# Second expert layer: second products with the weights held still and all tokens of an expert moving

## The chip, the cores and the metric

The kernel runs on one core of a Trainium2 chip. TensorE (PE) multiplies: the fixed operand is loaded into the array first (its weight load, PEld), then the moving operand is streamed through it column by column, and the sums gather in one of eight banks. VectorE (DVE) and ScalarE (ACT) read those banks and write SBUF, GpSimd (POOL) issues the indirect transfers, and SyncE (SP) issues the loads of weights. Each engine works through its own instructions in the order in which they were issued and meets the others at semaphores. The metric is the device time of one execution in microseconds (us).

## The reference, cut to what matters

Attention over 4 x 12 heads gives 1792 tokens of 768 features, and a first expert layer transforms them. The second expert layer, which is what changes, gives every token to one of 8 experts, 224 tokens to each (`cap`), greedily by logit, and applies two products with a relu between them:

```python
    cap = N // E
    ...
    out = np.zeros((N, D), dtype=np.float32)
    for e in range(E):
        mask = assigned == e
        h = np.maximum(x[mask] @ w1[e], 0.0)
        out[mask] = h @ w2[e]
    return out.astype(np.float32)
```

Here N is 1792, D is 768 and the hidden width F is 1024.

## The kernel before

The second expert layer is the function `moe2`. It takes the experts one after the other. One expert has 32 steps (the loop over `t` at L2420): steps 0 to 15 are the first products, steps 16 to 31 the second ones.

**Tokens in.** The 224 tokens of an expert are gathered from `y` in two halves of 112 rows (`gather`, L2277, one indirect transfer each, on POOL) and turned by TensorE so that features lie on the partitions (`turn`, L2284 to L2300: 4 groups of 3 transposes, L2293, then copies on ACT, L2297, and DVE, L2300). The four groups are called g0 to g3 below; g0 and g1 are the first half of the tokens, g2 and g3 the second. The turned tokens are `xx`.

**First products.** A tile of w1 (128 x 128) is the fixed operand and all 224 tokens move. Experts 0 and 1 (`NAT` = 2) use plain 4-byte numbers, and TensorE makes two instructions of each such matmul (`acc`, L2308). Experts 2 to 7 use split numbers, a high and a low part of each operand: one matmul over 448 columns (tokens high and low, with the high weights, L2316) and one over 224 columns (tokens high, with the low weights, L2317), together `acc2`. The result goes through relu into `ht` (experts 0 and 1) or, by `relu2` (L2319 to L2329: ACT, DVE, ACT, DVE), into the high part `hh` and the low part `hl`.

**Second products.** `gemm2` (L2335) does it the other way round: the fixed operand is a piece of the hidden values (128 x 112 tokens), and 384 columns of w2 move. Per step it does two units; a unit is one plain matmul (L2345) or three split ones (L2348 to L2350). An expert has 32 units. The result has tokens on the partitions, so it is copied by ACT (L2355) and scattered to `out` by POOL (L2356) as it stands. The sums lie in three banks, `po3` = bank4, bank5 and bank6.

**Weights.** For experts 2 to 7 the weights come in 14 pieces each (6 of w1, 8 of w2) through a ring of 6 buffers (`qkv`). Each piece is split by `split` (L2266 to L2275): the high part by ACT (L2272, `w1h`, `w2h`), the low part by DVE (L2274, `w1l`, `w2l`). The splits of w1 for the next expert are done in the second phase of this one. Pieces 3 to 5 of an expert's w1 are held back (`LATE`, L2253 to L2257, a one-element MEMSET on POOL) until the gather of that expert's tokens has been issued.

**What sets the order.** The instruction order is written out by the program in advance: a planner (`Pace`, L1541) keeps an estimated clock for each engine, and the work that decides which tokens the next experts get (the assigner: many small instructions on PE, DVE and ACT, ending in `ids`, L2067) is put between the products where the planner's clocks have room. `ahead` (L2407) puts the gathers, turns and w1 splits of the next expert in where their planned inputs are there. The order is fixed when the program is built; an engine never takes a later instruction first.

Of the kernel before, what the change touches and what calls it, by code (L numbers as in the profile page):

```python
# [20 lines left out]
CP, NC = 112, 4  # L21
# [506 lines left out]
class Router:  # L528
# [15 lines left out]
    def init(self):  # L544
# [32 lines left out]
        self.i128 = pool.tile([CP, 1, 128], F32, name="i128")  # L577
# [141 lines left out]
    def first_slot(self, tb):  # L719

        nc, work = self.tc.nc, self.work
        na = (NB - 1) * NC
        shp = [CP, na, E]
        t = work.tile(shp, F32, name="fst")
        nc.vector.tensor_tensor(out=t, in0=self.oh[:, :na, :], in1=self.nst[:CP].to_broadcast(shp), op=OP.mult)
        p = work.tile([CP, na], F32, name="fsp")
        nc.vector.tensor_reduce(out=p, in_=t, axis=AX.X, op=OP.add)
        nc.vector.scalar_tensor_tensor(p, p, float(BIG), self.pl[:, :na], op0=OP.mult, op1=OP.add)
        os = []
        for n in range(NB + 1):  # L730
            yield
            if n < NB - 1:
                os.append([work.tile([CP, 128], F32R, name="fso", bufs=2 * NC) for _ in range(NC)])
                for j in range(NC):
                    nc.vector.tensor_scalar(os[n][j], self.i128[:, 0, :], p[:, n * NC + j : n * NC + j + 1], None, op0=OP.is_equal)
            m = n - 2
            for j in range(NC if m >= 0 else 0):
                nc.tensor.matmul(tb[:, 4 * m : 4 * m + 4], lhsT=os[m][j], rhs=self.tr[:, m * NC + j, :], start=j == 0, stop=j == NC - 1)
        yield
        t0 = work.tile([128, 1, 4], F32, name="t0")  # L740
        nc.vector.tensor_reduce(out=t0[:, 0, :], in_=tb.rearrange("p (n i) -> p i n", i=4), axis=AX.X, op=OP.add)
        self.slot0 = self.rows(1, t0[:, :, 0], (t0[:, :, 1], t0[:, :, 2]), "0")

    def slots(self, tb, room, ones):
# [76 lines left out]
        for j in range(na):  # L821
            o = ones[j][:CP] if j < len(ones) else work.tile([CP, 128], F32R, name="slo", bufs=3)
            if j in ON_ACT:

                sq = room[3][:CP, 128 * (j % 8) : 128 * (j % 8) + 128]
                nc.scalar.activation(sq, self.i128[:, 0, :], AF.Square, scale=-1.0, bias=lo[:, j : j + 1])
                nc.scalar.activation(o, sq, AF.Relu, scale=-1.0, bias=one)
            else:
                nc.vector.tensor_scalar(o, self.i128[:, 0, :], lo[:, j : j + 1], None, op0=OP.is_equal)
# [775 lines left out]
class Assigner:  # L1605
# [11 lines left out]
    def __init__(self, tc, consts, pool, bank, y, l2):  # L1617
# [27 lines left out]
        self.i128 = tile("i128a", [128, 128])  # L1645
        nc.gpsimd.iota(self.i128, pattern=[[1, 128]], base=0, channel_multiplier=0, allow_small_or_imprecise_dtypes=True)
# [517 lines left out]
def moe2(tc, consts, qkv, x0, asn, w1, w2, y, out):  # L2164
# [10 lines left out]
    with ExitStack() as ctx:  # L2175
# [11 lines left out]
        hl = p2.tile([128, KF, CAP], F32R, name="hl")  # L2187
        rows = {}
        zr = x0[0]
# [11 lines left out]

        def result(n, h, i):
            return po3[(4 * n + 2 * h + i) % 3][:CP, :384]
# [115 lines left out]
        def relu2(pg, f):  # L2319
            hr, hh = rows["hr"][f % NHR], rows["hh"]  # L2320
# [14 lines left out]
        def gemm2(n, h, t):  # L2335
            ts = slice(h * CP, (h + 1) * CP)

            todo = [(0, 0), (0, 1)] if t == 0 else [(1, 0), (1, 1)] if t == 1 else [(0, t), (1, t)]
            for i, k in todo:
                po = result(n, h, i)  # L2340
                work("p", 0.646 if n < NAT else 0.528, max(there[n, False, k], there["h", k]))
                cs = slice(384 * i, 384 * i + 384)
                ht, hh = rows["ht"], rows.get("hh")
                if n < NAT:
                    nc.tensor.matmul(po, lhsT=ht[:, k, ts], rhs=ws[n][1][:, k, cs], start=k == 0, stop=k == KF - 1)  # L2345
                else:
                    w2h, w2l = wh["2"]
                    nc.tensor.matmul(po, lhsT=hh[:, k, ts], rhs=w2h[:, k, cs], start=k == 0, stop=False)  # L2348
                    nc.tensor.matmul(po, lhsT=hh[:, k, ts], rhs=w2l[:, k, cs], start=False, stop=False)  # L2349
                    nc.tensor.matmul(po, lhsT=hl[:, k, ts], rhs=w2h[:, k, cs], start=False, stop=k == KF - 1)  # L2350

        def store(n, h):
            work("s", 0.98)
            for i in range(2):
                nc.scalar.activation(zr[:CP, 384 * i : 384 * i + 384], result(n, h, i), AF.Copy)  # L2355
            nc.gpsimd.indirect_dma_start(out=out, out_offset=IndirectOffsetOnAxis(ap=asn.ids[:, n, h : h + 1], axis=0), in_=zr[:CP], in_offset=None)  # L2356
# [10 lines left out]
        def experts(compact):  # L2367
# [28 lines left out]
            for n in range(E):  # L2396
                turns, gathered, turned = [], 0, 0

                def ahead(t):
# [7 lines left out]
                    elif t >= 17:  # L2407
# [9 lines left out]
                        if what[0] == n + 1 and (what[1] or n >= NAT and t > 25 and what[2] <= t - 25) and nload > nsplit + direct and arrival[what] <= clock["p"] + EARLY:  # L2417
                            split(*what)

                for t in range(32):  # L2420
# [10 lines left out]
                    if n and t == 3:  # L2431
                        store(n - 1, 1)
                    if t == 25:
                        store(n, 0)
# [19 lines left out]
                    else:  # L2454
                        gemm2(n, (t - 16) // 8, t % 8)
# [21 lines left out]
            store(E - 1, 1)  # L2477
# [15 lines left out]
NHR = 5  # L2493
# [5 lines left out]
NHR = 5  # L2499
# [7 lines left out]
ON_POOL = 4  # L2507
FEW = 7
# [3 lines left out]
def fused_kernel(tc, q, k, v, g_q, g_k, modality_id, w_gate, bias, w1, w2, w_gate2, w12, w22, out):  # L2512
    nc = tc.nc
    with ExitStack() as ctx:
# [13 lines left out]
        x0 = (xp.tile([128, DM], F32, name="x0"), xp.tile([128, KD, 128], F32R, name="xh"), xp.tile([128, KD, 128], F32R, name="xl"))  # L2528
# [40 lines left out]
```

## Time and profile before

| what | value |
|---|---|
| median of 3 runs (lowest, highest) | 993.45 us (989.86, 994.93) |
| the profiled execution | 989.51 us |
| its span, from the first to the last instruction | 987.6 us |
| mean granted TensorE clock, share of full speed | 0.994 |
| TensorE busy | 955.5 us, 97% of the span |
| VectorE busy | 655.4 us, 66% |
| ScalarE busy | 506.5 us, 51% |
| `moe2` | from about 665 us to the end |

The profile lists for each engine how long it was busy, what ended its idle time, and, in the trace, the start and length of every instruction. Matmuls overlap: the length of one is longer than the distance to the next, so costs on TensorE are read from the starts, not from the lengths. In the timelines P stands below for the start of an expert's first second product; the trace has P = 829.02 for expert 3, 862.58 for expert 4, 896.31 for expert 5 and 929.46 for expert 6.

### The profile page before, as it was taken

Reading aid. Unit: us, or ns where it says so; the run is one execution under the profiler, and the core shown is the slowest. Engines: PE = TensorE matmul, PEld = TensorE weight load, DVE = VectorE, ACT = ScalarE, POOL = GpSimd, SP = SyncE. Lnnn points to the kernel's source line nnn. Section 1 sums busy time; section 2 is a strip of 40 time slices with the busy share of each in tenths; the row PEclk is TensorE's granted clock in tenths of the full one; section 3 lists DMA queues with packets and bytes.
Section 4 is the critical chain, followed back from the end, with each engine's and each line's share of the span. In section 5 each row is a group of like instructions: output and inputs, shape, how many; then the busy total and the mean of one; then the engine's idle time right before and its main releaser. Section 6 shows DMA issues by size and latency. Waiting matters only on the chain. (4 is left out here: it accounts for less than half of the span.)

```text
span 987.6 us, 19357 instructions
## 1 busy us (share of the span) xinstructions
PE 955.5 (97%) x6241; PEld 774.6 (78%) x6241; DVE 655.4 (66%) x1693; ACT 506.5 (51%) x1158; POOL 306.8 (31%) x456
## 2 busy tenths in 40 slices
PE   7999999999999999999999999989999999999996
PEld 6666677677666688888888998747667799999996
DVE  6676877877965664444666554677778877687660
ACT  4787788788784422222441222741214466576651
POOL 4877776777632410100060111010110210220100
PEclk9999999999999999999999999999999999999999
DMA  7676577667465353728621111016932386767631
GB/s 164 144 159 165 145 167 175 152 161 173 97 194 183 113 210 113 252 88 303 231 84 34 34 65 38 18 47 248 343 126 80 117 274 217 251 209 243 217 114 31
DMA packets 81036, 152.55 MB, mean 154 GB/s; under 512 B 14270, under 2 KB 53438, under 8 KB 80768
## 3 DMA queue, kind: packets, MB, share of 16 engines
q1 hardware_dynamic: 73568, 127.57, 43.5%
q0 software_dynamic: 5200, 23.33, 7.4%
q8 instruction: 54, 0.88, 0.4%
q14 instruction: 86, 0.70, 0.2%
q10 hardware_dynamic: 2128, 0.07, 0.1%
HBM read 112.27 MB, written 17.44 MB: 131 GB/s over the span
## 5 line engine op out<-in xcount | busy, mean ns | idle before, releaser
L238 ACT ACTIVATE e<-sp,nm 112x448 f32<-112x448 f32 x192 | 123.6, 644 | 36.7 <-DVE nm L232 33.8
L232 DVE TENSOR_REDUCE nm<-sp 112x1 f32<-112x448 f32 x192 | 115.9, 616 | 27.5 <-PE sp L231 26.5
L1100 DVE CUSTOM_DVE_ANT_0 prod<-po,wgb,gt 128x384 bf16<-128x384 f32 x96 | 93.0, 969 | 37.8 <-ACT yr L1324 34.4
L246 PEld LDWEIGHTS tp<-ident,e 112*112 112x112 f32 x768 | 86.0, 134 | 38.8 <-DVE rs L277 6.3
L246 PE MATMUL tp<-ident,e 112*112 112x112 f32 x768 | 107.2, 262 | 3.6 <-ACT et L252 3.5
L2316 PE MATMUL bank<-xx,w1h 128*128 128x448 f32 x288 | 92.6, 378 | 0.0
L252 ACT ACTIVATE et<-tp 112x448 f32<-112x448 f32 x142 | 78.2, 551 | 16.6 <-PE tp L246 16.6
L230 PE MATMUL sp<-bt,at 128*112 128x448 f32 x188 | 82.9, 441 | 0.8 <-DMA bt<-cut 0.8
L1036 PE MATMUL po<-w2h,hh 128*128 128x384 f32 x224 | 78.9, 352 | 0.1
L2356 POOL DMA_INDIRECT out_dram<-x,ids x16 | 16.4, 1024 | 200.4 <-ACT x L2355 166.5
L1013 PE MATMUL pg<-w1h,xh 128*128 128x512 f32 x180 | 75.0, 417 | 3.0 <-ACTq L970 2.1
L259 PE MATMUL op<-et,qkv 112*64 112x448 f32 x384 | 77.5, 545 | 0.0
L2317 PE MATMUL bank<-xx,w1l 128*128 128x224 f32 x288 | 76.5, 265 | 0.0
L1037 PE MATMUL po<-w2l,hh 128*128 128x384 f32 x224 | 75.2, 336 | 0.1
L1038 PE MATMUL po<-w2h,hl 128*128 128x384 f32 x224 | 75.2, 336 | 0.0
L1014 PE MATMUL pg<-w1l,xh 128*128 128x512 f32 x180 | 71.2, 396 | 0.0
L1015 PE MATMUL pg<-w1h,xl 128*128 128x512 f32 x180 | 71.2, 395 | 0.0
L231 PE MATMUL sp<-bt,qz 128*112 128x448 f32 x188 | 69.2, 368 | 0.0
L2348 PE MATMUL bank<-w2h,hh 128*112 128x384 f32 x192 | 66.3, 345 | 0.0
L2350 PE MATMUL bank<-w2h,hl 128*112 128x384 f32 x192 | 64.7, 337 | 0.0
L2349 PE MATMUL bank<-w2l,hh 128*112 128x384 f32 x192 | 64.6, 337 | 0.0
L1136 POOL DMA_INDIRECT y<-yr,ti x11 | 11.4, 1039 | 161.3 <-POOLq L970 113.4
(485 smaller groups left out, 2277.0 us busy)
## 6 DMA issues: line engine op xcount, KB each, us to landing
qkv<-in_moe_w_dram SPq DMA_DIRECT2D x88, 384.0 KB
qkv<-in_moe_w_dram SPq DMA_DIRECT2D x36, 512.0 KB
raw<-in_moe_w_dram SPq DMA_DIRECT2D x24, 512.0 KB
bt<-cut SPq DMA_DIRECT2D x96, 112.0 KB
at<-cut SPq DMA_DIRECT2D x96, 112.0 KB
w1s<-in_moe_w_dram SPq DMA_DIRECT2D x12, 512.0 KB
w2s<-in_moe_w_dram SPq DMA_DIRECT2D x16, 384.0 KB
qkv<-in_v_dram SPq DMA_DIRECT2D x12, 448.0 KB
```

Source lines behind the costliest of these rows:

```text
L230: nc.tensor.matmul(sp, lhsT=at[:, h, cs], rhs=bt[:, h, :], start=True, stop=False)
L232: nc.vector.tensor_reduce(out=st["nm"][:, n : n + 1], in_=sp, axis=AX.X, op=OP.max, negate=True)
L238: nc.scalar.activation(e, st.pop(("s", n)), AF.Exp, bias=st["nm"][:, n : n + 1], accum_out=st["sm"][:, n : n + 1])
L246: nc.tensor.transpose(tp[:, kc, :], e[:, kc * CP : (kc + 1) * CP], ident[:CP, :CP])
L252: nc.scalar.activation(dst, tp, AF.Copy)
L259: nc.tensor.matmul(st["op"][h * D : (h + 1) * D, :], lhsT=raws[i // 2][:, 2, 2 * (i % 2) + h, kc * D : (kc + 1) * D], rhs=st["et"][:, h, k ...
L1036: nc.tensor.matmul(po[n], lhsT=hh[:, k, :], rhs=w2h[:, kk, cs], start=kk == 0, stop=False)
L1037: nc.tensor.matmul(po[n], lhsT=hh[:, k, :], rhs=w2l[:, kk, cs], start=False, stop=False)
L1038: nc.tensor.matmul(po[n], lhsT=hl[:, k, :], rhs=w2h[:, kk, cs], start=False, stop=kk == KF - 1)
L1100: nc.vector.tensor_tensor_reduce(out=prod, in0=y, in1=wgb[:, cs, e], scale=gt, scalar=init[:, e : e + 1] if init is not None else 0.0, op0 ...
L2316: nc.tensor.matmul(pg, lhsT=h[:, k, fs], rhs=xx[:, k].rearrange("p a c -> p (a c)"), start=k == 0, stop=False)
L2317: nc.tensor.matmul(pg[:, :CAP], lhsT=l[:, k, fs], rhs=xh[:, k, :], start=False, stop=k == KD - 1)
```

## The change

For experts 0 to 6 the second product is turned round: a 128 x 128 tile of w2 is the fixed operand, and all 224 tokens move (`second`), in 48 units per expert (6 blocks of 128 output features, d, by 8 pieces of the hidden width, k), three units per step, in the order `UNITS`. A unit is one plain matmul over 224 columns, or for split experts one over 448 columns (`hh` and `hl` now lie side by side in one tile, `hx`) and one over 224. Each block d fills one bank of `po3`, `po3[d % 3]`, for its 8 units.

The result then has features on the partitions. `leave` copies it to `yt`: ACT alone for experts 0 and 1; for split experts ACT copies one half of the sum to a small buffer `hr` and DVE adds the other half from the bank. The bank is free for block d + 3 only after that. `back` turns `yt` on TensorE into rows of tokens (4 groups of 3 transposes per expert: two in steps 28 and 30, two in steps 4 and 6 of the next expert), and `keep` copies them by ACT and scatters them. Blocks 4 and 5 leave in the next expert's step 0. The last expert keeps `gemm2`. Splits of w2 for the next expert are let in by `FREE2` in place of a fixed step, the ring of `hr` has 3 buffers in place of 5, there are two `zr` for the rows on their way out, and one constant (`i128`) is shared.

```diff
-        def gemm2(n, h, t):
+        def gemm2(h, t):
...
+        def second(n, d, k):
+            ds = slice(128 * d, 128 * d + 128)
+            po = po3[d % 3]
+            flags = dict(start=k == 0, stop=k == KF - 1)
+            done["y", d] = work("p", 0.388 if n < NAT else 0.318, max(there[n, False, k], there["h", k]))
+            if n < NAT:
+                nc.tensor.matmul(po[:, :CAP], lhsT=ws[n][1][:, k, ds], rhs=rows["ht"][:, k, :], **flags)
+            else:
+                w2h, w2l = wh["2"]
+                hx = rows["hx"][:, k]
+                nc.tensor.matmul(po[:, : 2 * CAP], lhsT=w2h[:, k, ds], rhs=hx.rearrange("p a c -> p (a c)"), start=k == 0, stop=False)
+                nc.tensor.matmul(po[:, :CAP], lhsT=w2l[:, k, ds], rhs=hx[:, 0], start=False, stop=k == KF - 1)
+
+        def leave(n, d):
+            po, to = po3[d % 3], yt[:, d]
+            if n < NAT:
+                work("s", 0.36, done["y", d])
+                nc.scalar.activation(to, po[:, :CAP], AF.Copy)
+                return
+            hr = rows["hr"][d % NHR]
+            t = work("s", 0.36, done["y", d])
+            nc.scalar.activation(hr, po[:, CAP : 2 * CAP], AF.Copy)
+            work("v", 0.39, t)
+            nc.vector.tensor_tensor(out=to, in0=po[:, :CAP], in1=hr, op=OP.add)
+
+        def back(h, i, px):
+            work("p", 0.33)
+            for k in range(3):
+                nc.tensor.transpose(px[:CP, 128 * k : 128 * k + 128], yt[:, 3 * i + k, h * CP : (h + 1) * CP], ident)
+
+        def keep(n, h, i, px):
+            work("s", 0.49)
+            nc.scalar.activation(zr[h][:CP, 384 * i : 384 * i + 384], px[:CP, :384], AF.Copy)
+            if i:
+                nc.gpsimd.indirect_dma_start(out=out, out_offset=IndirectOffsetOnAxis(ap=asn.ids[:, n, h : h + 1], axis=0), in_=zr[h][:CP], in_offset=None)
...
-                        if what[0] == n + 1 and (what[1] or n >= NAT and t > 25 and what[2] <= t - 25) and nload > nsplit + direct and arrival[what] <= clock["p"] + EARLY:
+                        if what[0] == n + 1 and (what[1] or n >= NAT and t > FREE2[what[2]]) and nload > nsplit + direct and arrival[what] <= clock["p"] + EARLY:
...
-                        gemm2(n, (t - 16) // 8, t % 8)
+                        if n + 1 == E:
+                            gemm2((t - 16) // 8, t % 8)
+                        else:
+                            for u in range(3 * t - 48, 3 * t - 45):
+                                second(n, *UNITS[u])
...
-NHR = 5
+NHR = 3
...
+UNITS = [(2 * j + d, k) for j in range(3) for d, k in [(0, 0), (0, 1), (1, 0), (1, 1)] + [(d, k) for k in range(2, 6) for d in range(2)] + [(0, 6), (0, 7), (1, 6), (1, 7)]]
+LEAVES = [u // 3 + 1 for d in range(6) for u in (UNITS.index((d, 7)),)]
+FREE2 = [16 + max(UNITS.index((d, k)) for d in range(4, 6)) // 3 for k in range(8)]
+TURNED, TURNED2 = (28, 30), (4, 6)
```

The rows below are instructions as they stand on one engine, in order; `waits` names the engines whose semaphores an instruction waits for.

TensorE, expert 3, second phase, before: two units around the turn group g2 (xg1).

```order
L2348 MATMUL bank5_11540<-w2h_12740,hh_12745 112x384
L2349 MATMUL bank5_11540<-w2l_12741,hh_12745 112x384
L2350 MATMUL bank5_11540<-w2h_12740,hl_11544 112x384
L2293 MATMUL bank7_11542<-ident_71,xg1_11546 128x112 [waits DMASW3_49,DVE_49]
L2293 MATMUL bank7_11542<-ident_71,xg1_11546 128x112 x2
L2348 MATMUL bank4_11539<-w2h_12740,hh_12745 112x384
```

The same place after: units 15 to 19; bank6 is block d = 2, and the second bank4 is block d = 3.

```order
L2289 MATMUL bank7_11540<-ident_71,xg1_11545 128x112 [waits DMASW2_49,DVE_49]
L2289 MATMUL bank7_11540<-ident_71,xg1_11545 128x112 x2
L2355 MATMUL bank5_11538<-hx_12803,w2h_12798 128x448
L2356 MATMUL bank5_11538<-hx_12803,w2l_12799 128x224
L2355 MATMUL bank6_11539<-hx_12803,w2h_12798 128x448
L2356 MATMUL bank6_11539<-hx_12803,w2l_12799 128x224
L2355 MATMUL bank6_11539<-hx_12803,w2h_12798 128x448
L2356 MATMUL bank6_11539<-hx_12803,w2l_12799 128x224
L2355 MATMUL bank4_11537<-hx_12803,w2h_12798 128x448 [waits DVE_49]
L2356 MATMUL bank4_11537<-hx_12803,w2l_12799 128x224
```

Unit 18, the first of block 3, now waits for a DVE instruction, the one that empties bank4 of block 0.

VectorE, expert 3, second phase, before: the splits of the next expert's w1 (w1l) and its turned tokens (xx).

```order
L2274 TENSOR_TENSOR w1l_12328<-qkv1_87,w1h_12327 128x1024
L2300 TENSOR_TENSOR xx_11543<-bank7_11542,xx_11543 128x3x112
L2274 TENSOR_TENSOR w1l_12328<-qkv1_87,w1h_12327 128x1024
L2274 TENSOR_TENSOR w1l_12328<-qkv0_86,w1h_12327 128x1024
L2300 TENSOR_TENSOR xx_11543<-bank2_11537,xx_11543 128x3x112
L2274 TENSOR_TENSOR w1l_12328<-qkv0_86,w1h_12327 128x1024 x2
```

The same place after.

```order
L2270 TENSOR_TENSOR w1l_12348<-qkv1_87,w1h_12347 128x1024
L2296 TENSOR_TENSOR xx_11541<-bank7_11540,xx_11541 128x3x112
L2270 TENSOR_TENSOR w1l_12348<-qkv1_87,w1h_12347 128x1024
L2270 TENSOR_TENSOR w1l_12348<-qkv0_86,w1h_12347 128x1024
L2296 TENSOR_TENSOR xx_11541<-bank2_11535,xx_11541 128x3x112
L2270 TENSOR_TENSOR w1l_12348<-qkv0_86,w1h_12347 128x1024
L2368 TENSOR_TENSOR yt_11543<-bank4_11537,hr0_12804 128x224
L2270 TENSOR_TENSOR w1l_12348<-qkv0_86,w1h_12347 128x1024
L2368 TENSOR_TENSOR yt_11543<-bank5_11538,hr1_12805 128x224
```

The add that empties bank4 (the first yt, L2368) stands behind four w1l and two xx.

VectorE, the numbers of expert 7's tokens (ids), before: amid expert 5's first products, between the hr and hl of its relu.

```order
L2324 TENSOR_TENSOR hr0_12746<-bank7_11542,hr0_12746 128x224
L2329 SCALAR_TENSOR_TENSOR hl_11544<-hr0_12746,hh_12745 128x224
L2063 TENSOR_TENSOR table_11116<-table_11116,bank1_11536 112x32
L2064 TENSOR_TENSOR sel_11155<-table_11116,full_11105 112x32
L2065 TENSOR_REDUCE sum4_11156<-sel_11155 112x4
L2067 TENSOR_TENSOR ids_11118<-sum4_11156 112x2
L2324 TENSOR_TENSOR hr1_12747<-bank2_11537,hr1_12747 128x224
```

After: in expert 6's second phase, the whole stretch from the first three w1l on.

```order
L2270 TENSOR_TENSOR w1l_12348<-qkv1_87,w1h_12347 128x1024 x2
L2270 TENSOR_TENSOR w1l_12348<-qkv0_86,w1h_12347 128x1024
L2368 TENSOR_TENSOR yt_11543<-bank4_11537,hr0_12804 128x224
L2368 TENSOR_TENSOR yt_11543<-bank5_11538,hr1_12805 128x224
L2062 TENSOR_TENSOR table_11116<-table_11116,bank1_11534 112x32
L2063 TENSOR_TENSOR sel_11153<-table_11116,full_11105 112x32
L2064 TENSOR_REDUCE sum4_11154<-sel_11153 112x4
L2066 TENSOR_TENSOR ids_11118<-sum4_11154 112x2
L2368 TENSOR_TENSOR yt_11543<-bank6_11539,hr2_12806 128x224
L2368 TENSOR_TENSOR yt_11543<-bank4_11537,hr0_12804 128x224
L2296 TENSOR_TENSOR xx_11541<-bank7_11540,xx_11541 128x3x112
L2270 TENSOR_TENSOR w1l_12348<-qkv0_86,w1h_12347 128x1024
```

The ids moved from the first phase of one expert to the second phase of the next, behind three w1l; likewise the ids of expert 6 moved from expert 4's first phase to expert 5's second one. The gathers, the turns and pieces 3 to 5 of w1 follow them.

TensorE at the end of expert 6's second phase, before: the last unit and expert 7's first products.

```order
L2348 MATMUL bank4_11539<-w2h_12740,hh_12745 112x384
L2349 MATMUL bank4_11539<-w2l_12741,hh_12745 112x384
L2350 MATMUL bank4_11539<-w2h_12740,hl_11544 112x384
L2316 MATMUL bank2_11537<-xx_11543,w1h_12327 128x448 [waits DVE_49]
L2317 MATMUL bank2_11537<-xx_11543,w1l_12328 128x224
```

After: the last units, g2 and g3, and expert 7's first products.

```order
L2355 MATMUL bank6_11539<-hx_12803,w2h_12798 128x448
L2356 MATMUL bank6_11539<-hx_12803,w2l_12799 128x224
L2289 MATMUL bank7_11540<-ident_71,xg1_11545 128x112 [waits DMASW0_49,DVE_49]
L2289 MATMUL bank7_11540<-ident_71,xg1_11545 128x112 x2
L2289 MATMUL bank2_11535<-ident_71,xg1_11545 128x112 [waits DVE_49]
L2289 MATMUL bank2_11535<-ident_71,xg1_11545 128x112 x2
L2312 MATMUL bank2_11535<-xx_11541,w1h_12347 128x448 [waits DVE_49]
L2313 MATMUL bank2_11535<-xx_11541,w1l_12348 128x224
```

Here g2 and g3 stand behind all second products, directly ahead of the first product that reads them; before, all four groups stood between units in the first half of the phase.

## Rows read from the trace of the kernel before

**Rows 1.** Page of the profile, part 1: busy time, share of the span, instructions.

```profile
PE 955.5 (97%) x6241; PEld 774.6 (78%) x6241; DVE 655.4 (66%) x1693; ACT 506.5 (51%) x1158; POOL 306.8 (31%) x456
```

**Rows 2.** Waits of TensorE, 665 to 990 us: in total, times, longest us.

```profile
PE bank L2293 <- DMA xg<-y,ids: 2.0, 2, 1.1
PE bank L2293 <- DVE hl L2329: 0.8, 1, 0.8
```

**Rows 3.** Timeline of TensorE, expert 6, where its phases start: start us, us, line.

```profile
929.46 0.34 PE L2348 MATMUL bank<-w2h,hh 128*112 128x384 f32 x1
...
947.43 0.36 PE L2316 MATMUL bank<-xx,w1h 128*128 128x448 f32 x1
...
962.61 0.34 PE L2348 MATMUL bank<-w2h,hh 128*112 128x384 f32 x1
```

**Rows 4.** Timeline of TensorE, transposes between second products of experts 2 and 1.

```profile
773.57 0.81 PE L2345 MATMUL bank<-w2s,ht 128*112 128x384 f32 x2
774.22 0.49 PE L1824 MATMUL bank<-ident,bid 128*128 128x128 f32 x3
774.54 0.81 PE L2345 MATMUL bank<-w2s,ht 128*112 128x384 f32 x2
...
797.08 0.34 PE L2350 MATMUL bank<-w2h,hl 128*112 128x384 f32 x1
797.26 0.45 PE L2293 MATMUL bank<-ident,xg 112*128 112x112 f32 x3
...
797.72 0.34 PE L2349 MATMUL bank<-w2l,hh 128*112 128x384 f32 x1
```

**Rows 5.** Timeline of TensorE, plain products of experts 0 and 1.

```profile
689.01 3.65 PE L2308 MATMUL bank<-xtt,w1s 128*128 128x224 f32 x18
692.49 0.49 PE L2060 MATMUL bank<-place,g 128*112 128x32 bf16 x7
...
758.50 2.75 PE L2345 MATMUL bank<-w2s,ht 128*112 128x384 f32 x8
761.08 0.45 PE L2293 MATMUL bank<-ident,xg 112*128 112x112 f32 x3
```

**Rows 6.** Timeline of VectorE, second phase of expert 6.

```profile
931.90 1.23 DVE L2274 TENSOR_TENSOR w1l<-qkv,w1h 128x1024 fp32r<-128x1024 f32 x1 [0.56 <-ACT w1h L2272]
...
933.46 2.35 DVE L2274 TENSOR_TENSOR w1l<-qkv,w1h 128x1024 fp32r<-128x1024 f32 x2
...
936.15 2.35 DVE L2274 TENSOR_TENSOR w1l<-qkv,w1h 128x1024 fp32r<-128x1024 f32 x2
938.41 0.50 DVE L2300 TENSOR_TENSOR xx<-bank,xx 128x336 fp32r<-128x336 f32 x1
```

**Rows 7.** Groups of instructions, 672 to 988 us: busy us, mean ns, idle before.

```profile
L2272 ACT ACTIVATE w1h<-qkv 128x1024 fp32r<-128x1024 f32 x36 | 36.6, 1051 | 0.0
...
L2324 DVE TENSOR_TENSOR hr<-bank,hr 128x224 f32<-128x224 f32 x48 | 18.7, 390 | 17.1 <-ACT hr L2322 17.0
L2322 ACT ACTIVATE hr<-bank 128x224 f32<-128x224 f32 x48 | 17.2, 359 | 32.7 <-PE bank L2317 32.6
```

**Rows 8.** Timeline of VectorE, expert 7's numbers in expert 5's first phase.

```profile
893.91 0.18 DVE L2063 TENSOR_TENSOR table<-table,bank 112x32 f32<-112x32 f32 x1
...
894.59 0.16 DVE L2067 TENSOR_TENSOR ids<-sum 112x2 int32<-112x2 f32 x1
```

**Rows 9.** Landing of two gathers (663.4, 916.2 us), and POOL's timeline around the second.

```profile
DMA to landing us min/median/max: 3.7/3.7/3.7
...
DMA to landing us min/median/max: 7.0/7.0/7.0
...
916.16 0.97 POOL L2282 DMA_INDIRECT xg<-y,ids  x1 [0.16 <-issue]
...
918.39 0.09 POOL L2257 MEMSET qkv<- 1x1 f32 x1
```

**Rows 10.** Stretch by stretch: PE, PEld, DVE, ACT, POOL busy, clock, DMA share, GB/s.

```profile
922.00:926.00 4.00, 4.00 (x28) 3.77 (x27) 1.57 (x4) 1.58 (x5) 0.00 (x0) 1.00 1.00 332
```

More of the change, by code (lines that the diff above doesn't have):

```diff
@@ L2342, in gemm2 @@
                 cs = slice(384 * i, 384 * i + 384)
[L2343 to L2356, printed above, removed]
+                hh, hl = rows["hx"][:, k, 0, ts], rows["hx"][:, k, 1, ts]
+                nc.tensor.matmul(po, lhsT=hh, rhs=w2h[:, k, cs], start=k == 0, stop=False)
@@ new lines, in gemm2 @@
+                nc.tensor.matmul(po, lhsT=hh, rhs=w2l[:, k, cs], start=False, stop=False)
+                nc.tensor.matmul(po, lhsT=hl, rhs=w2h[:, k, cs], start=False, stop=k == KF - 1)
+        def second(n, d, k):
[6 more added lines that the diff above has]
+            else:
+                w2h, w2l = wh["2"]
+                hx = rows["hx"][:, k]
+                nc.tensor.matmul(po[:, : 2 * CAP], lhsT=w2h[:, k, ds], rhs=hx.rearrange("p a c -> p (a c)"), start=k == 0, stop=False)
+                nc.tensor.matmul(po[:, :CAP], lhsT=w2l[:, k, ds], rhs=hx[:, 0], start=False, stop=k == KF - 1)
@@ new lines, in keep, with results @@
+        def keep(n, h, i, px):
[3 more added lines that the diff above has]
+                nc.gpsimd.indirect_dma_start(out=out, out_offset=IndirectOffsetOnAxis(ap=asn.ids[:, n, h : h + 1], axis=0), in_=zr[h][:CP], in_offset=None)
+        def results(n, t):
+            if n + 1 < E and t in TURNED:
+                back(TURNED.index(t), 0, pg2[1])
+            if n + 1 < E and t - 1 in TURNED:
+                keep(n, TURNED.index(t - 1), 0, pg2[1])
+            if n + 1 < E and t - 16 in LEAVES:
+                leave(n, LEAVES.index(t - 16))
+            if n and t + 16 in LEAVES[4:]:
+                for d in range(4, 6):
+                    if LEAVES[d] == t + 16:
+                        leave(n - 1, d)
+            if n and t in TURNED2:
+                back(TURNED2.index(t), 1, po3[TURNED2.index(t)])
+            if n and t - 1 in TURNED2:
+                keep(n - 1, TURNED2.index(t - 1), 1, po3[TURNED2.index(t - 1)])
@@ L2430, in experts @@
                         next(sums, None)
[L2431 to L2434, printed above, removed]
+                    results(n, t)
+                    if n + 1 == E and t == 25:
+                        for i in range(2):
+                            keep(n, 0, i, po3[i])
                     ahead(t)
@@ L2464, in experts @@
                     wh["2"] = tiles(1, "right", *((i, (KF, DM), F32R) for i in ("w2h", "w2l")))
-                    rows["hh"], *rows["hr"] = tiles(1, "right", ("hh", (KF, CAP), F32R), *((f"hr{i}", (CAP,), F32) for i in range(NHR)))
+                    rows["hx"], *rows["hr"] = tiles(1, "right", ("hx", (KF, 2, CAP), F32R), *((f"hr{i}", (CAP,), F32) for i in range(NHR)))
                 while known <= n + 1:
@@ L2476, in experts @@
                     split(*piece(nsplit + direct))
-            store(E - 1, 1)
+            for i in range(2):
+                keep(E - 1, 1, i, po3[(2 + i) % 3])
             for r in room:
@@ L2498 @@
 FIRST = 1
-NHR = 5
+NHR = 3
 LATE = 3
```

25 lines of the change are left out of this document (11 added, 14 removed).

## Prediction

> **What bounds the kernel now.** I read the busy times first: TensorE is busy for 97% of the span, VectorE for 66%, ScalarE for 51% [rows 1]. Then the waits of TensorE in the expert layer that changes: 2.8 us in all between 665 and 990 us, in three pieces [rows 2]. So here TensorE's own instructions set the time, and every microsecond taken from them counts, as long as nothing makes TensorE wait; every new wait counts in full too. The third view is the timeline of one split expert: its second phase runs from 929.46 to 947.43 us, its neighbour's first products from there to 962.61 [rows 3]. Those two stretches give the prices of the old and of the new form, since the new second products have the shapes of the first ones (a 128 x 128 tile held, 448 and 224 columns moving).
>
> **What is removed and added on TensorE.** The 48 first pairs take 962.61 - 947.43 = 15.18 us, 0.316 each [rows 3]. The second phase takes 17.97 us; it holds 4 turn groups of three transposes. One such group stands between the starts 797.08 and 797.72 together with two matmuls; at the ordinary distance of 0.175 (525 ns per unit of three) that leaves 0.64 - 0.35 = 0.29 for the group [rows 4]. Without them 17.97 - 4 x 0.29 = 16.8 us remain, 32 units of 0.525. So a split expert's second products go from 16.8 to 15.2 us, a gain of 1.6; for experts 2 to 6 that is 8.1.
>
> For the plain experts, where a matmul is two instructions, 8 instructions of the old form take 761.08 - 758.50 = 2.58 us, 0.3225 per instruction and 0.645 per unit; 18 instructions of the first products take 3.48 us, 0.193 each and 0.387 per matmul [rows 5]. 32 x 0.645 = 20.6 becomes 48 x 0.387 = 18.6: a gain of 2.1 each, 4.2 for experts 0 and 1. The whole gain is 12.3 us.
>
> The turning back adds 7 x 4 = 28 groups of three transposes against the 4-byte identity. The nearest row is a group of three of the same kind and width (128 moving columns) between plain products: from 773.57 to 774.54 with two products of 0.3225 in it, so 0.97 - 0.645 = 0.32 [rows 4]; the narrower groups (112 columns) gave 0.29. I take 0.32: 28 x 0.32 = 9.0 us (8.1 to 9.2). TensorE's own work thus falls by 12.3 - 9.0 = 3.3 us.
>
> The Trainium skill, "TensorE: Matmul & The Clock Gate", section "Back-to-back issue gap", gives a distance of N/2.4 + 2.5 ns for an isolated matmul of N columns at the full clock; it also says that in a stream the weight loads count. By that formula an old split unit would take 0.488 and a new pair 0.285 us, where the rows show 0.525 and 0.316. The gain per split expert would be 1.9 in place of 1.6, the sum 1.6 us lower; I go by the rows.
>
> **What is moved to other engines.** ACT gets, per split expert, 6 copies out of the banks of 0.36 [rows 7] and keeps its 4 row copies; DVE gets 6 adds of 0.39 [rows 7]. Neither engine is full over a whole expert, so as busy time I cost them at nothing. What counts is their place in the queue, as the block that fills a bank for the second time waits for the add that emptied it.
>
> **The first new wait: bank4, unit 18.** Unit 18 opens block 3 in the bank of block 0 and waits for DVE. On DVE the add of block 0 stands behind the fourth split of the next expert's w1 in experts 2, 3 and 4. In the trace of expert 6, which has the same string of splits and turned tokens before the change as those, the first split starts 2.44 us after P (929.46), the fourth at 936.15, and two take 2.26, so the fourth ends at P + 7.82 [rows 3, 6]. The add ends at P + 8.2, and TensorE goes on at P + 8.3. It arrives earlier: 18 units of 0.316 and three turn groups of 0.29 are 6.56. So it waits for 1.75 us in experts 3 and 4. In expert 2 the wait for `hl` of 0.8 [rows 2] makes it arrive later, so 0.95. In experts 5 and 6 only three splits stand ahead: the add is done by P + 6.2, TensorE is there at 5.7 to 6.0 with a few small products of the assigner between, and waits for about 0.3. Together 0.95 + 3.5 + 0.6 = 5.05. The bounds: no wait, if the splits ran some 1.8 us earlier than now (they start when ACT's `w1h` is done [rows 6], and nothing in the change moves that), and 6.5 if experts 2, 5 and 6 paid more. The later banks have room: bank6 for block 5 is the tightest, some 0.1 us.
>
> **The second new wait: the next expert's tokens, experts 5 and 6.** The planner counts the new adds on DVE and so puts the assigner's last steps later. The `ids` of expert 7, now amid expert 5's first products at 894.59 [rows 8], come in expert 6's second phase behind three splits and two adds: P + 2.44 + 3 x 1.13 + 2 x 0.39 + the 0.84 from `table` to the end of `ids` [rows 6 to 8] = P + 7.5. The two gathers follow; 2.2 us after the first the gate for pieces 3 to 5 of w1 opens [rows 9], at P + 9.9. What a transfer then needs is not shown for this place. In a quiet queue a gather landed after 3.7 us, in one shared with weight loads after 7.0 [rows 9]. At P + 7.5 the queue of weights is held at the gate, so I take 3.7 for the first gather: it lands at P + 11.4, and TensorE wants it at about P + 12.0. With 3.7 for the first of the three held pieces too, and 0.52 MB at 332 GB/s [rows 10] = 1.55 for each more, the last lands at P + 16.7; then ACT splits it for 1.05 [rows 7] and DVE for 1.22 [rows 6], to P + 19.0. Behind that, by the order, comes the DVE step for g2 (0.5), without which expert 7's first product can't start: P + 19.6. TensorE is done with the second products and all its transposes at 15.2 + 1.9 (6 groups: two back, four in) + 0.3 = P + 17.4. The wait is 2.2, and by the same steps 2.0 for expert 5 (`ids` earlier by one add, one w2 split more ahead of g2). I take 2.1 each, 4.2 together. Its bounds are 1.2 each, if the pieces land as they are wanted and only DVE's order counts, and about 4 each with the landing of 7.0, where TensorE already stops at g0 (P + 7.2 + 7.0 = 14.2 against 10.8 in expert 5).
>
> Other moves at nothing: the stores are issued by POOL behind gathers that have no hurry, and `out` is stored later by some steps, but expert 7 keeps the old end. Three `hr` buffers serve a chain of 0.85 us per block. The back transposes in the next expert's steps 4 and 6 come more than 1 us after block 5's add.
>
> **The sum.** -12.3 + 9.0 + 5.05 + 4.2 = +5.95 us. On the profiled execution (989.51, span 987.6) that is 995.5. The median of the runs shown is 993.45, 3.9 above the profiled one; the forecast is made for the median: 999.4.
>
> **The rivals.**
> *No new wait.* If DVE reaches the add before TensorE reaches unit 18 (P + 6.56; it needs to be 1.75 us ahead of the trace) and the next tokens come in time, only TensorE's own work counts: -3.3, 990.1 us. This is the one that ends on the other side, though within 0.5%. For it: with the same splits on DVE TensorE waits for only 2.8 us now. Against: the splits' times are measured, and the order puts the add behind them.
> *Only the bank waits.* If the held pieces and the gathers land early, or DVE's order has more slack at the expert's end than I see: -3.3 + 5.05 = +1.75, 995.2.
> *A late gather.* At the landing of 7.0 both experts 5 and 6 pay about 4 in place of 2.1: +9.8, 1003.2. For it: the row at 916.16 stands ahead of the same gate. Against: there the loads of w1 ran beside it, which now come later.
> *Dear transposes.* The same page of the Trainium skill, section "Part 4: PE-mode transpose", gives about 275 ns for a transpose in a kernel's context and says that such work doesn't count toward the clock. At 0.275 each in place, 84 transposes cost 23.1 in place of 9.0: +20, 1013.5. The rows speak against it: three between products took 0.29 to 0.32 in all [rows 4].
>
> **How the numbers follow.** The forecast with both waits, 997 to 1002, has 0.48; only the bank waits 0.20; no new wait 0.10; a late gather 0.15; dear transposes 0.02; something below all of them 0.05. A measurement of this kernel tells about 0.5% (5 us) from no change. Faster by more than that, below 988.5, is 0.06. Within it lie the two cheap cases and the lower edge of the forecast (up to 998.4): 0.38. Slower has 0.56. The range from 991.0 to 1004.5 leaves out the no-wait case and the dearest ones, about 2 in 10.
>
> **What would show it.** Right: pairs of second products 0.316 apart; turn-back groups costing 0.32; unit 18 of experts 3 and 4 waiting about 1.75 us for the first `yt` add behind the fourth w1l; the first product of experts 6 and 7 waiting about 2 us for `xx`. Wrong: TensorE's waits in the layer staying near 2.8 us, w1l starting earlier than P + 2.4, or g0 of experts 6 and 7 waiting for its gather.

## The result, and the profile after

The changed kernel takes 1003.88 us (median of 6 runs, 1002.17 to 1006.51) against 993.26 us (median of 6) before on the same chip. These medians lie 10.6 us apart; the ratio given with the result is 1.0134, with an interval of 1.0113 to 1.0154, which is 13 us. It is slower, as forecast, but by 11 to 13 us, not by 6. The profiled execution took 1002.17 us with a span of 1000.3.

The page of the kernel after, part 1, and TensorE's waits from 660 to 1000 us (in total, times, longest us), which answer to [rows 1, 2]. Waits and phases, here and below, are read from one trace of each kernel:

```profile
PE 957.7 (96%) x6389; PEld 790.7 (79%) x6389; DVE 663.1 (66%) x1723; ACT 514.3 (51%) x1200; POOL 304.6 (30%) x455
```

```profile
PE bank L2312 <- DVE xx L2296: 5.0, 2, 2.7
PE bank L2355 <- DVE yt L2368: 4.1, 3, 1.5
PE bank L2373 <- ACT x L2377: 1.5, 1, 1.5
PE bank L2289 <- DVE xx L2296: 1.4, 1, 1.4
PE bank L2289 <- DMA xg<-y,ids: 1.3, 2, 1.1
```

TensorE is busy for hardly longer, but waits for 13.3 us where it waited for 2.8. Four kinds of wait are new: the first product of experts 6 and 7 for `xx`, unit 18 for the `yt` add, a turn-back group (L2373) for ACT's copy of the one ahead, and a turn group (L2289) for `xx`.

Where the time went is read best from the starts of the phases. The table gives the length of each phase in us, from its first product to the first product of the next; F are first and S second products, e1 and e2 two of the experiments below.

| phase | before | after | e1_early_ids | e2_spread |
|---|---|---|---|---|
| experts 0 and 1, S | 29.39, 25.09 | 26.64, 23.33 | 26.64, 23.33 | 26.64, 23.32 |
| expert 2, F and S | 15.30, 19.35 | 16.26, 18.66 | 16.26, 20.79 | 16.24, 19.29 |
| expert 3, F and S | 16.83, 17.97 | 17.71, 18.67 | 15.95, 18.89 | 15.83, 17.77 |
| expert 4, F and S | 15.59, 18.13 | 15.95, 18.80 | 16.25, 19.02 | 15.83, 17.43 |
| expert 5, F and S | 15.60, 17.96 | 15.84, 22.62 | 16.25, 18.79 | 15.84, 17.04 |
| expert 6, F and S | 15.19, 17.97 | 17.38, 22.21 | 15.84, 18.79 | 15.83, 17.03 |
| expert 7, F and S | 15.19, 25.02 | 18.01, 24.91 | 15.84, 24.90 | 15.83, 25.08 |
| from expert 0's first product to the end | 315.1 | 328.2 | 318.8 | 310.2 |

Up to the end of expert 4 the changed kernel is a little ahead: expert 5 starts at 879.35 in place of 880.71 us. From expert 5's second phase on it loses 14 us, in four phases.

The timeline of TensorE after (start us, us, engine, line, operation, and in brackets the idle time before it with what ended it), around the end of expert 5:

```profile
907.48 0.38 PE L2355 MATMUL bank<-hx,w2h 128*128 128x448 f32 x1
907.69 0.27 PE L2356 MATMUL bank<-hx,w2l 128*128 128x224 f32 x1
907.80 0.38 PE L2355 MATMUL bank<-hx,w2h 128*128 128x448 f32 x1
...
912.28 0.54 PE L2373 MATMUL bank<-ident,yt 128*112 128x128 f32 x3 [1.49 <-ACT x L2377]
...
917.81 0.74 PE L2312 MATMUL bank<-xx,w1h 128*128 128x448 f32 x1 [2.33 <-DVE xx L2296]
...
918.53 0.60 PE L2312 MATMUL bank<-xx,w1h 128*128 128x448 f32 x1
918.93 0.39 PE L2313 MATMUL bank<-xx,w1l 128*128 128x224 f32 x1
919.12 0.60 PE L2312 MATMUL bank<-xx,w1h 128*128 128x448 f32 x1
...
921.56 0.38 PE L2312 MATMUL bank<-xx,w1h 128*128 128x448 f32 x1
```

A pair of second products takes 0.32 us, as foreseen. Then come a wait of 1.49 and, at the start of expert 6's first products, one of 2.33; and behind it the pairs stand 0.59 apart (918.53 to 919.12) until about 921. That is not a wait. The stretches say what it is (busy time of each engine, granted clock, DMA share, GB/s):

```profile
894.00:917.60 23.60, 19.79 (x132) 17.59 (x131) 16.29 (x46) 12.69 (x22) 1.99 (x3) 1.00 0.53 181
917.80:921.00 3.20, 3.19 (x11) 2.98 (x12) 2.29 (x4) 0.48 (x2) 0.00 (x0) 0.50 0.97 331
921.20:934.60 13.40, 13.40 (x89) 12.72 (x88) 9.60 (x20) 8.97 (x21) 2.89 (x3) 1.00 0.48 157
...
957.40:961.80 4.40, 4.40 (x15) 4.10 (x16) 3.26 (x6) 1.54 (x5) 0.00 (x0) 0.50 0.90 308
```

The granted clock is 0.50, the lower of its two levels (1.2 in place of 2.4 GHz), from 917.6 to 921.0 and again from 955.1 to 961.9: the first time as the wait of 2.33 ends, the second from within the wait of 2.71 at the next expert's end, 0.9 us behind one of 1.40. In the kernel before it is 1.00 all through these phases.

What held expert 6's tokens and weights back is on ACT, DVE and POOL, same kernel, same stretch, one fence for each engine in this order; the last lines of ACT and POOL are the first held piece and the gate of expert 7:

```profile
910.79 1.06 ACT L2268 ACTIVATE w1h<-qkv 128x1024 fp32r<-128x1024 f32 x1 [2.98 <-DMA qkv<-in_moe_w_dram]
911.75 0.47 ACT L2377 ACTIVATE x<-bank 112x384 f32<-112x384 f32 x1
...
951.39 1.06 ACT L2268 ACTIVATE w1h<-qkv 128x1024 fp32r<-128x1024 f32 x1 [2.75 <-DMA qkv<-in_moe_w_dram]
```

```profile
901.05 0.39 DVE L2368 TENSOR_TENSOR yt<-bank,hr 128x224 f32<-128x224 f32 x1
...
902.03 0.16 DVE L2066 TENSOR_TENSOR ids<-sum 112x2 int32<-112x2 f32 x1
...
911.88 1.23 DVE L2270 TENSOR_TENSOR w1l<-qkv,w1h 128x1024 fp32r<-128x1024 f32 x1 [2.97 <-ACT w1h L2268]
...
916.84 0.92 DVE L2296 TENSOR_TENSOR xx<-bank,xx 128x336 fp32r<-128x336 f32 x2
```

```profile
902.98 0.96 POOL L2278 DMA_INDIRECT xg<-y,ids  x1 [11.66 <-PE bank L2356]
904.25 0.95 POOL L2278 DMA_INDIRECT xg<-y,ids  x1 [0.30 <-issue]
905.19 0.09 POOL L2253 MEMSET qkv<- 1x1 f32 x1
...
945.48 0.09 POOL L2253 MEMSET qkv<- 1x1 f32 x1
```

The numbers (`ids`) are there at P + 7.0 (P = 895.19), the first gather starts 0.8 us later, the gate for the held pieces of w1 opens at 905.19, and the first held piece is there at 910.79, 5.6 us later (5.9 for expert 7: 945.48 to 951.39). ACT stands still for 2.98 us until then, and with it its own later work: the copy of the turn-back group (911.75), for whose bank TensorE waited until 912.28. DVE stands still for 2.97 us, and the last `xx` comes at 917.7, 2.3 us after TensorE wanted it.

Between the gate and the piece, from 905.3 to 910.8 us, the transfers were these (queue, packets, MB, busy share):

```profile
q1 hardware_dynamic: 240, 0.91, 45.8%
q0 software_dynamic: 145, 0.60, 42.1%
```

q1 brings the weights, q0 the gathers. The rest of the two gathers, 0.60 MB, came beside the pieces, and before 907 us only q0 moved anything.

### The profile page after: what moved, and what is told of

It reads as the page before. It is cut to its first block, busy times and chain, and to the rows that moved or that the text cites. A ratio compares the mean times of both kernels' runs of the same rounds, so it can differ in the third digit from the quotient of the medians.

```text
span 1000.3 us, 19728 instructions
## 1 busy us (share of the span) xinstructions
PE 957.7 (96%) x6389; PEld 790.7 (79%) x6389; DVE 663.1 (66%) x1723; ACT 514.3 (51%) x1200; POOL 304.6 (30%) x455
## 3 DMA queue, kind: packets, MB, share of 16 engines
q0 software_dynamic: 5200, 23.33, 7.4%
## 5 line engine op out<-in xcount | busy, mean ns | idle before, releaser
L2312 PE MATMUL bank<-xx,w1h 128*128 128x448 f32 x288 | 97.7, 391 | 5.0 <-DVE xx L2296 5.0
L2355 PE MATMUL bank<-hx,w2h 128*128 128x448 f32 x240 | 80.9, 387 | 4.2 <-DVE yt L2368 4.1
L2312 PEld LDWEIGHTS bank<-xx,w1h 128*128 128x128 f32 x288 | 56.0, 194 | 11.0 <-DVE xx L2296 5.5
L2356 PE MATMUL bank<-hx,w2l 128*128 128x224 f32 x240 | 63.7, 265 | 0.0
L259 PEld LDWEIGHTS op<-et,qkv 112*64 112x64 f32 x384 | 25.5, 136 | 41.0 <-issue 41.0
```

Of the source, the lines that this page charges most:

```text
L259: nc.tensor.matmul(st["op"][h * D : (h + 1) * D, :], lhsT=raws[i // 2][:, 2, 2 * (i % 2) + h, kc * D : (kc + 1) * D], rhs=st["et"][:, h, k ...
L2312: nc.tensor.matmul(pg, lhsT=h[:, k, fs], rhs=xx[:, k].rearrange("p a c -> p (a c)"), start=k == 0, stop=False)
L2355: nc.tensor.matmul(po[:, : 2 * CAP], lhsT=w2h[:, k, ds], rhs=hx.rearrange("p a c -> p (a c)"), start=k == 0, stop=False)
```

## The experiments

The theory after the result (A, D): the waits at the ends of experts 5 and 6 come from the late numbers and the gate behind them, they form one chain, and the half clock follows from the waits. The rivals: the transposes or the new products lower the clock or cost more by themselves (B), holding the splits back costs elsewhere (C), each wait has a cause of its own (E), the late gather matters and not the held pieces (F).

### The planner's charge taken out

```diff
             t = work("s", 0.36, done["y", d])
             nc.scalar.activation(hr, po[:, CAP : 2 * CAP], AF.Copy)
-            work("v", 0.39, t)
             nc.vector.tensor_tensor(out=to, in0=po[:, :CAP], in1=hr, op=OP.add)
```

> The changed kernel with one line of the planner taken out: the DVE add of leave is not charged to the planner's DVE clock, so the numbers of experts 6 and 7's tokens are made in the first phases of experts 4 and 5 again, as before the change. Theory A (the late numbers caused the waits at the ends of experts 5 and 6, and those waits caused the two stretches at half clock): no wait at the ends, no half clock between 700 us and the last expert, unit 18 waits 1.3 to 1.8 us in all five split experts: -3.3 + 5 x 1.5 = +4 us against the kernel before, ratio 1.004. Rival B (the new transposes or the new form lower the clock or cost more by themselves): half clock stays in the layer and the ratio stays at 1.010 or more.

Measured: ratio 1.0013 (0.9985 to 1.0041); the layer takes 318.8 us, 3.7 more than before, where 4 were expected (the expected ratio of 1.004 lies at the upper end of the interval). TensorE's waits in the layer:

```profile
PE bank L2355 <- DVE yt L2367: 7.5, 5, 1.6
PE bank L2289 <- DMA xg<-y,ids: 1.1, 1, 1.1
```

Five waits of unit 18 and nothing at the ends, and the clock stays full in the layer until 5 us before its end. So the transposes and the new products don't lower it, and the order alone, by one number of the planner, cost the 9.4 us of the layer between this kernel and the changed one.

### The splits spread

```diff
-what[0] == n + 1 and (what[1] or n >= NAT and t > FREE2[what[2]])
+what[0] == n + 1 and (what[1] and (n < NAT or t > (16, 16, 22, 22, 27, 27)[what[2]]) or not what[1] and n >= NAT and t > FREE2[what[2]])
```

This is on top of the first experiment.

> As e1_early_ids, and the splits of the next expert's w1 are held back so that two stand ahead of the first add of leave, two between the second and third, two behind the fourth. Theory A: the wait of unit 18 goes too (two splits and two xx end at P + 5.6, the add at P + 6.0, TensorE arrives at P + 6.5), TensorE's own work remains: -3.3 us, ratio 0.997, within 0.5%. Rival C (the splits held back come late for the next expert's first products, or w2's are pushed): a new wait of 1 us or more per expert at the first products, ratio 1.002 or more.

Measured: 986.07 us, ratio 0.9944 (0.9917 to 0.9970). It is 0.6% faster than the kernel before, and faster than the changed one. No wait for DVE is left in the layer:

```profile
PE bank L2289 <- DMA xg<-y,ids: 1.0, 1, 1.0
```

The layer takes 310.2 us, 4.9 less than before; 3.3 were expected. Against e1_early_ids the five waits of unit 18 cost 8.6 us, 7.5 of idle time and about 0.2 each for the start after it. The held splits made no new wait: the first phases of experts 3 to 7 take 15.83 us, 0.64 more than the 15.19 that they take before at their shortest, which is their two turn-back groups.

### Only the plain experts in the new form

```diff
+NEW = range(0, 2)
...
-                        if n + 1 == E:
-                            gemm2((t - 16) // 8, t % 8)
+                        if n not in NEW:
+                            gemm2(n, (t - 16) // 8, t % 8)
```

Copies, stores and the limit on w2's splits follow the same condition.

> Only experts 0 and 1 have the new form; experts 2 to 6 keep the old products, copies and stores. By the terms of the sum: 2 x (20.6 - 18.6) = 4.2 gained, 8 groups of transposes at 0.32 = 2.6 paid, no add on DVE, no wait: -1.6 us, ratio 0.998. Were a transpose 0.275 us in place, 24 of them would cost 6.6 and the result would be +2.4.

Measured: ratio 0.9948 (0.9921 to 0.9976); the layer takes 311.7 us, 3.4 less than before, where 1.6 were expected. The sign is the theory's. Of the 1.8 us beyond it, 0.4 is in the products: from start to start they took 22.70 us before and 20.43 here in expert 0, 21.34 and 18.98 in expert 1, a gain of 4.6 in place of 4.2. The rest is waits of the kernel before that the sum had left standing: the one of 0.8 for `hl` in expert 2 [rows 2] is gone, and the one for `xg` in expert 0's second phase fell from 1.08 to 0.52. By the traces e2_spread is 1.5 us shorter than this kernel: 0.6 of it in expert 0's second phase, where the rest of that wait is gone, and 0.9 from expert 2's second phase on, where the prediction's terms give 5 x (1.6 - 4 x 0.32) = 1.6 for the split experts. The runs don't show this difference: the medians are 985.22 here and 986.07 in e2_spread.

### Waits by measure, in the kernel before

```diff
+                    if t == 0 and n in STALL:
+                        v = hl[:, 6:8, :].rearrange("p a c -> p (a c)")
+                        for _ in range(STALL[n]):
+                            nc.vector.tensor_tensor(out=v, in0=v.bitcast(F32), in1=v.bitcast(F32), op=OP.max)
+                        nc.vector.tensor_copy(out=xl[:, 0, 0:1], in_=xl[:, 0, 0:1].bitcast(F32))
...
+STALL = {3: 2, 5: 4, 7: 8}
```

> The kernel before with TensorE made to wait at three starts of first products: chains of 2, 4 and 8 extra DVE steps of about 0.55 us between the last second product and the first first product of experts 3, 5 and 7 (waits of about 1.4, 2.5 and 4.7 us). Theory A: the clock is halved for some microseconds behind the waits of 2.5 and 4.7 us, as behind the waits of the changed kernel, and not behind 1.4. Rival B (the clock fell for another reason, such as the transposes): full clock behind all three.

The waits came out longer than meant. TensorE's first products behind them:

```profile
815.31 0.47 PE L2316 MATMUL bank<-xx,w1h 128*128 128x448 f32 x1 [2.18 <-DVE xx L2441]
...
889.94 0.74 PE L2316 MATMUL bank<-xx,w1h 128*128 128x448 f32 x1 [4.35 <-DVE xx L2441]
...
966.09 0.74 PE L2316 MATMUL bank<-xx,w1h 128*128 128x448 f32 x1 [6.67 <-DVE xx L2441]
```

and the stretches behind the first one, by the columns above:

```profile
813.00:816.80 3.80, 1.62 (x10) 1.41 (x10) 3.13 (x7) 0.01 (x1) 3.10 (x4) 1.00 0.42 123
816.90:820.20 3.30, 3.30 (x15) 2.56 (x14) 1.53 (x3) 2.13 (x5) 0.00 (x0) 0.50 1.03 368
820.40:833.00 12.60, 12.60 (x88) 11.21 (x87) 6.48 (x22) 4.60 (x14) 0.92 (x1) 1.00 0.53 191
```

In the kernel before, which has no turn-back, the clock falls to half behind all three waits: for 3.4 us behind 2.18, for 6.8 us from within 4.35 and 6.67. As none of the three was short, this run alone doesn't part length from place. The next one does.

`STALL = {3: 0, 4: 1, 5: 0, 6: 1}`, otherwise the same edit:

> The kernel before with shorter waits at four starts of first products: no extra DVE step in experts 3 and 5, one in experts 4 and 6, beside the short step that rewrites a part of the tokens. By the longer chains (2.3 us with two steps of 0.55, 4.5 with four) the waits should be about 1.2, 1.7, 2.3 and 2.8 us. Theory A: the clock stays full behind the waits below about 1.6 us (as behind the five of 1.3 to 1.6 at unit 18) and is halved for some microseconds behind those of 2.3 and more. Rival B (what counts is the place, the start of first products, not the length of the wait): half clock behind all four.

```profile
818.96 0.47 PE L2316 MATMUL bank<-xx,w1h 128*128 128x448 f32 x1 [1.16 <-DVE xx L2441]
...
857.12 0.74 PE L2316 MATMUL bank<-xx,w1h 128*128 128x448 f32 x1 [3.09 <-DVE xx L2441]
...
894.31 0.47 PE L2316 MATMUL bank<-xx,w1h 128*128 128x448 f32 x1 [1.65 <-DVE xx L2441]
...
930.85 0.47 PE L2316 MATMUL bank<-xx,w1h 128*128 128x448 f32 x1 [2.71 <-DVE xx L2441]
```

```profile
819.00:822.00 3.00, 3.00 (x21) 2.56 (x21) 1.22 (x4) 0.84 (x2) 2.19 (x3) 1.00 0.69 202
857.20:860.40 3.20, 3.20 (x11) 2.98 (x12) 0.55 (x2) 0.00 (x0) 1.15 (x3) 0.50 0.94 357
894.40:897.50 3.10, 3.10 (x20) 2.92 (x21) 1.05 (x5) 1.00 (x3) 1.99 (x3) 1.00 0.74 209
932.30:935.50 3.20, 3.20 (x12) 2.99 (x12) 1.12 (x2) 1.85 (x5) 0.60 (x2) 0.50 1.03 392
```

Full clock behind 1.16 and 1.65 us, half behind 3.09 and 2.71, all at the same kind of place. Rival B falls. A half stretch of 3.4 us makes the first products of an expert 1.65 us longer (expert 4: 17.24 in place of 15.59). In the changed kernel expert 6's first products were 17.38 us against 15.84 of the same instructions at full clock in e1_early_ids, 1.54 more.

Length isn't all of it, though. Ahead of this layer every trace has one wait of 2.15 to 2.17 us in a full stream, at the same instruction. In the kernel before the clock stays full behind it (first line and its stretch); in the changed kernel it falls (second pair):

```profile
615.93 0.50 PE L1013 MATMUL pg<-w1h,xh 128*128 128x512 f32 x1 [2.15 <-ACTq L970]
615.90:619.30 3.40, 3.37 (x17) 2.77 (x18) 2.91 (x14) 0.00 (x0) 2.65 (x12) 1.00 0.03 7
...
613.84 0.80 PE L1013 MATMUL pg<-w1h,xh 128*128 128x512 f32 x1 [2.15 <-ACTq L970]
613.90:617.10 3.20, 3.20 (x8) 2.55 (x9) 2.82 (x14) 0.00 (x0) 2.59 (x12) 0.50 0.01 3
```

Of the ten traces three have half clock there: the changed kernel, e2_spread and e7_stall_small. What decides it at this length no run here shows.

### The second turn-back group in a bank of its own

```diff
-                back(TURNED.index(t), 0, pg2[1])
+                back(TURNED.index(t), 0, (pg2[1], po3[0])[TURNED.index(t)])
```

> The changed kernel, but the second turn-back group of an expert goes to bank4 (po3[0], free by then) in place of bank3, where it waited 1.5 us in expert 5 for ACT's copy of the first group. That copy stood behind a w1h that waited for its weights. Theory D (the ends of experts 5 and 6 are set by one chain: gate, loads of w1 pieces 3 to 5, w1h, w1l, xx): the wait of 1.5 goes and the wait of the next first product grows from 2.3 to about 3.8; time within 0.3% of the changed kernel, ratio to the kernel before 1.011 to 1.015. Rival E (the waits add up, each with a cause of its own): 1.5 us less, ratio about 1.011 or below, and 2.3 stays.

Measured: ratio 1.0159 (1.0118 to 1.0200), 1005.45 us: no gain over the changed kernel, and a little above the 1.011 to 1.015 of theory D, into which the interval reaches. The waits at the end of expert 5:

```profile
917.29 0.51 PE L2289 MATMUL bank<-ident,xg 112*128 112x112 f32 x3 [1.82 <-DVE xx L2296]
...
920.13 0.61 PE L2312 MATMUL bank<-xx,w1h 128*128 128x448 f32 x1 [2.33 <-DVE xx L2296]
```

The wait of 1.49 is gone, and one of 1.82 stands at the next turn group in its place; the last 2.33 is the same. So rival E falls, and theory D holds, though not at the place that it named: the time came back not at the first product but one step earlier in the same chain.

### The gate left open

```diff
-                    nc.gpsimd.memset(r[0:1, 0:1], 0.0)
+                    if n < 6:
+                        nc.gpsimd.memset(r[0:1, 0:1], 0.0)
```

> The changed kernel with the same order on every engine, but the one-element MEMSET that holds pieces 3 to 5 of w1 of experts 6 and 7 back until their gathers are issued is left out. Theory D: the pieces are there early, ACT's w1h no longer waits, the waits at the ends of experts 5 and 6 fall from 8.1 us to under 3, no half clock follows, and the time falls by 8 to 10 us, to a ratio near 1.004. Rival F (the late gather is the cause, not the pieces): loads beside the gather make it land after 7 to 9 us in place of 3.8, TensorE waits 3 to 5 us for xg at g0, and the time stays near the changed kernel's.

Measured: ratio 1.0057 (1.0034 to 1.0080), 997.2 us. The waits at the ends of experts 5 and 6:

```profile
916.85 0.47 PE L2313 MATMUL bank<-xx,w1h 128*128 128x448 f32 x1 [1.08 <-DVE xx L2297]
...
952.99 0.48 PE L2313 MATMUL bank<-xx,w1h 128*128 128x448 f32 x1 [2.32 <-DVE xx L2297]
```

With the pieces early they are 1.08 and 2.32 and a gather wait of 0.5, 3.9 in place of 8.1, and half clock follows only the longer one. The first gather of each pair still lands in 4.1 and 3.9 us, so rival F falls: the held pieces were half of it. The other half goes with the late numbers too, since e1_early_ids has no wait at these places; that it is the place of g2 and g3 behind all second products is read from the order, and was not tried alone. Theory D had expected waits under 3 and no half clock: the gain was about 7 us (6.7 in the layer), not 8 to 10, as 3.9 of waits stayed and one half stretch with them.

### Without the turn-back

The transposes of `back` are left out, and `keep` copies from `yt`, on top of e2_spread.

> As e2_spread, with the 84 transposes of back left out and keep copying from the unturned yt, so that the rows of experts 0 to 6 in the output are not turned back. By the term of the sum (28 groups of 0.32) the expert layer is 9.0 us shorter than in e2_spread, 310.2 - 9.0 = 301.2 us; with transposes of 0.275 each in place it would be 23 us shorter, 287.

The layer takes 302.0 us (672.0 to 974.1), 8.2 less than e2_spread, where 9.0 were expected. TensorE has two waits for the assigner in this layer that e2_spread doesn't have:

```profile
PE bank L2080 <- DVE fb L2075: 0.4, 1, 0.4
PE bank L1979 <- DVE ns L1975: 0.3, 1, 0.3
```

With these 0.7 us taken off, the 28 groups account for 8.9 us, 0.32 each, as the term had it.

## Why the prediction was wrong

The sign and the places of both new waits were right, and the size was about half of what came. The measured time lies in the range only because that left room for a late gather, which is not what came. Two steps failed: the landing of the held pieces of w1, and the clock, which the sum put at nothing. By the steps:

- **Products and transposes.** The sum had 12.3 gained and 9.0 paid, -3.3. Without new waits it is -4.9 (e2_spread). The terms themselves came nearly as worked out: 4.6 in place of 4.2 for the plain experts (e3_plain_only); 32.86 in place of 33.16 us for expert 6's two phases in e2_spread, 0.30 where the terms give 0.32; and 0.32 for a group of transposes (e8_no_back). What the sum didn't count is that two waits of the kernel before, 1.08 for `xg` and 0.8 for `hl` [rows 2], would go. With all this the layer would be 5.6 shorter; the 0.7 between lies in the split experts, 0.9 in place of 1.6 (e3_plain_only), and is not assigned further. By the Trainium skill, "TensorE: Matmul & The Clock Gate", "Back-to-back issue gap", the estimate for a pair was 0.285; the trace has 0.316. (The 1.6 us that the prediction takes off the sum by it should be 5 x 0.3 = 1.5.) The 0.275 us that the same page of the Trainium skill, "Part 4: PE-mode transpose", gives for a transpose agrees with the recorded length of one, 0.272 at the median (L2373), but not with its cost in the stream, which is 0.11.
- **Unit 18.** 5.05 was the term; three waits of 1.3 to 1.5, 4.1 in all, came. In expert 3 (P = 825.93) the first split started at P + 2.32, the add ended at P + 8.1 and TensorE went on at P + 8.13, 0.1 to 0.2 earlier than worked out; from start to start the gap ahead of unit 18 is 1.58 us, of which the trace counts 1.32 as idle. In expert 2 the wait was 1.28, not 0.95, as the wait for `hl` ahead of it is gone. In experts 5 and 6 the add was done in time.
- **The next expert's tokens.** This is the term that was mis-sized: 4.2, and 8.1 came (2.33 + 1.49 + 0.18 in expert 5, 2.71 + 1.40 in expert 6). The landing of the gather was right, 3.8 and 4.0 us, and the gate nearly: P + 10.3 in expert 6 for P + 9.9 (itself 0.2 more than its terms, 7.5 + 2.2), and P + 10.0 in expert 5. Wrong was the landing of the held pieces, taken at 3.7 from the gather's row. The first came 5.6 and 5.9 us behind the gate, 1.9 and 2.2 later than taken, and these 4.1 account for the missing 3.9. The gather's row was no price for it: the pieces go through another queue and came in beside the rest of both gathers; which of the two made them late was not tried. The step also looked only at the last consumer, the first product, and left out what ACT has queued behind the waiting w1h, the copy of the turn-back. So the lateness reached TensorE at two places; by e5_own_bank this parts the wait and doesn't add to it.
- **The clock.** The prediction had no term for it. With the waits at the ends the granted clock fell to half for 3.4 and 6.8 us. It cost 1.54 us in expert 6's first products and 2.17 in expert 7's (18.01 against 15.84), 3.7 in all. No wait of 2 us stands in this layer before, and behind the one of 2.15 ahead of it the clock stayed full, so the trace of before gave it no sure price; but the forecast brought two such waits in and bounded them by no more than their length.
- **The sum as it came.** -4.9 + 4.1 + 8.1 + 3.7, and about 0.2 for the start behind each of 8 waits, is 12.6; measured in the layer, 328.2 - 315.1 = 13.1. The last 0.5 is not assigned.
- **The rivals.** The no-wait case is what e2_spread is, 0.9944 rather than 0.9967. The late gather gave nearly the right time for the wrong reason: the gather landed early, and it was the weights behind it that came late.

What stays open: which waits of about 2 us bring half clock. In this layer all ten of 2.18 us and more in the ten traces did, and none up to 1.65 that stood alone, nor the one of 1.82 in e5_own_bank in the 3 us behind it; but of the ten of 2.15 to 2.17 ahead of the layer only three did. Whether what TensorE does around a wait matters was not tried.

## What to carry to other kernels

Where an order is fixed by a planner, a new step costs what it displaces: one add charged at 0.39 us moved a chain of numbers, gathers and loads by half a phase and was worth 9 us, while the change without new waits was worth 5. Follow the displaced chain to all its consumers, and on each in-order engine that waits for it name what stands behind the waiting instruction. Bound a new wait of TensorE of some 2 us and more by more than its length: in this layer each of 2.18 us and more came with 3.4 us or more at half clock, some 1.6 us on top per 3.4; waits of 1.3 to 1.6 cost their length and about 0.2.

## What was not expected of the hardware

- TensorE's granted clock fell to 0.50 behind single waits of 2.18, 2.32, 2.33, 2.71 and 3.09 us in an else full stream, for 3.4 us each (6.8 us from within 4.35 and 6.67, and where waits of 1.40 and 2.71 followed each other), and not behind waits of 1.08 to 1.65 us. Behind one wait of 2.15 to 2.17, at the same instruction in every trace, it fell in three traces of ten.
- A weight piece of 0.52 MB needed 5.6 and 5.9 us from its gate to ACT, where the gather of one half of the tokens just before it, in another queue, landed after 3.8 and 4.0.
